# Reordering a batch's matrix products, joining cosine and sine, and moving stores to GpSimd's queue in an attention-and-mixer kernel

## The chip, the cores and the metric

The kernel runs on one core of a Trainium2 chip. The metric is the device time of one execution in microseconds, lower is better. An engine executes its own instructions in the order in which they stand in its queue, and waits for other engines and for transfers by semaphores. TensorE is called PE here (its weight loads PEld), VectorE DVE, ScalarE ACT, GpSimd POOL and SyncE SP.

## The reference

```python
kv  = einsum('bhsd,bhse->bhde', k, v)              # 8 batches, 8 heads, 576 tokens, 64
o   = einsum('bhsd,bhde->bhse', q, kv)
x   = o / sqrt(mean(o*o) + 1e-6) * g_norm          # -> (8, 576, 512)
th  = x @ w_theta
y   = w_tok_r @ (x*cos(th)) + w_tok_i @ (x*sin(th))   # along the tokens
u   = x + y
x   = u + relu(u @ w_ch)                            # first mixer
h   = relu(x.T @ w_tok1) @ w_tok2                   # along the tokens, 576 -> 256 -> 576
u   = x + h.T
out = u + relu(u @ w_ch1) @ w_ch2                   # 512 -> 1536 -> 512
```

## The kernel before

Products run in 16 bits with each operand split in a high and a low half, so each product is three matmuls (`mm3`, lines 82 to 84). There are two parts. The first goes batch by batch and ends with `u` of each batch in DRAM (`u2d`); the second (`mlp`) reads it back and does the last two products for eight chunks.

In the first part a batch passes through units, each a Python generator. `go(unit)` first moves every unit in flight one `yield` further, then starts the new one, so the source order is a software pipeline written out by hand. A planner then sets each engine's queue from this order by a simulated timeline, the earlier instruction in the program first.

The units, by name: `kv(o, part)` (product k,v in two parts), `attend(o, r)` for five row tiles r (q times kv on PE; square on ACT, sum on DVE, `pow` and a product on POOL, a product and a split on ACT and DVE, then a DMA transpose through SP), `rotate(o, r)` (x times w_theta on PE, then sine and cosine on ACT and the products and splits `zh`, `zl` on DVE; `rotate_last` for the last 64 tokens), `mix(o, c, dt)` (27 matmuls; c is one of two token chunks of 256 and 320 columns, dt one of four channel tiles; DVE adds the result to `R`, line 422, ACT writes the high half `uh`, line 423, DVE the low half `ul`, line 426), `channel(o, c, ct)` (12 matmuls on `uh` and `ul` of all four dt of its chunk; DVE adds to `R`, line 446, ACT and DVE split to `xs`, and after every second one SP issues a DMA transpose to `xt`, line 457), `token1(o, j, part)` (6 or 8 matmuls of 512 columns on `xt`; ReLU split to `hh` and `hl`), `token2(o, c, dt)` (6 matmuls; DVE adds to `R`, line 489, and after the last dt SP stores `R` to `u2d`, line 491). `weight` and `stash` prepare weights: `stash` loads four blocks of w_ch1 or w_ch2, decodes float64 words (`decode`), forms sums of blocks on POOL, splits them on ACT and DVE and stores them through SP (line 218). There are 24 stashes, handed out by `spare`, five in a round.

The order of a round of one batch (batches 2 to 5) was: eight `mix` units with the next batch's `attend` 2 to 4 and all five `rotate` among the first seven, eight `channel` units, the next-but-one batch's first `kv` part, four `token1` units, the second `kv` part, eight `token2` units with `attend` 0 and 1 of the next-but-one batch. Below, a unit is named by a letter and its indices: M for mix, C for channel, H for token1 and T for token2 (M13 is chunk 1, tile 3; H10 is part 1, j 0), K00 and K10 for the two kv parts, a2 for attend 2, r3 for rotate 3. The functions that the change touches, with the line numbers of the profile:

Of the kernel before, what the change touches and what calls it, by code (L numbers as in the profile page):

```python
# [10 lines left out]
F16 = mybir.dt.float16  # L11
# [17 lines left out]
def attn_mixer_kernel(  # L29
# [88 lines left out]
    def decode(val, raw, inplace=False):  # L118
# [6 lines left out]
        to = raw[..., 0] if inplace else bits  # L125
        nc.vector.scalar_tensor_tensor(to, raw[..., 0], 29, bits, ALU.logical_shift_right, ALU.bitwise_or)
        nc.vector.scalar_tensor_tensor(to, raw[..., 1], -(2**31), to, ALU.bitwise_and, ALU.bitwise_or)

    def weight(pool, w, row, col, part, n, hi, lo, scale, name, raw=None):

        val = pool.tile([P, n], F32, tag="val", name=f"{name}v")[:part]
        rows = slice(row, row + part)
        if w.dtype == F32:
            load(val, w[rows, col:col + n])
            yield
        else:
            if raw is None:
                raw = pool.tile([P, n, 2], I32, tag="raw", name=f"{name}r")[:part]
                load(raw.rearrange("p n w -> p (n w)"), w.bitcast(I32)[rows, 2 * col:2 * (col + n)])
            yield  # L140
            yield from decode(val, raw)
        if w is not w_theta and w is not w_ch1:
# [9 lines left out]

    def weight_tile(pool, w, pr, j, n, scale, name, col=0, raw=None):
        at = slice(col, col + n)
        return weight(pool, w, j * P, col, P, n, pr[0][:, j, at], pr[1][:, j, at], scale, f"{name}{col}_{j}", raw)
# [26 lines left out]
    def stash(w, name, rows, cols, dst):  # L182
# [4 lines left out]
        words = () if w.dtype == F32 else (2,)  # L187
        raw = wp[0].tile([P, 4, P, *words], I32 if words else F32, tag="raw", name=f"{name}r")
        t = wp[0].tile([P, 4, P], F32, tag="val", name=f"{name}s")
        for half, at in ((0, slice(0, 4, 3)), (1, slice(1, 3))):  # L190
            src = (w.bitcast(I32) if words else w)[rows[half]:rows[half] + P, :]
            n = 2 if words else 1
            src = src.rearrange("p (a n) -> p a n", a=2)[:, :, n * cols:n * (cols + P)]
            load(raw[:, at].rearrange("p a n w -> p a (n w)") if words else raw[:, at], src)
# [3 lines left out]
        val = raw  # L198
        if words:

            yield from decode(t.rearrange("p x n -> p (x n)"), raw.rearrange("p x n w -> p (x n) w"), True)
            val = raw[..., 0].bitcast(F32)
        yield

        nc.gpsimd.tensor_tensor(t[:, 1], val[:, 3], val[:, 2], ALU.add)
        nc.gpsimd.tensor_tensor(t[:, 3], val[:, 3], val[:, 0], ALU.subtract)
        nc.gpsimd.tensor_tensor(t[:, 2], t[:, 1], val[:, 0], ALU.subtract)
        nc.gpsimd.tensor_tensor(t[:, 0], val[:, 1], t[:, 2], ALU.subtract)
        nc.scalar.activation(hi[:, :3], val[:, :3], AF.Copy, scale=SW)
        yield  # L210
        nc.vector.scalar_tensor_tensor(lo[:, :3], val[:, :3], SW, hi[:, :3], ALU.mult, ALU.subtract)
        yield
        nc.scalar.activation(hi[:, 3:], t, AF.Copy, scale=SW)
        yield
        nc.vector.scalar_tensor_tensor(lo[:, 3:], t, SW, hi[:, 3:], ALU.mult, ALU.subtract)
        yield
        for d, src in zip(dst, (hi, lo)):
            nc.sync.dma_start(d, src)

    def stash_wide(g, k):  # L220
        return stash(w_ch1, f"wa{g}{k}_", (k * P, (DH + k) * P), g * P, [t[:, g, k] for t in wad])

    def stash_narrow(g, m):
        return stash(w_ch2, f"wb{g}{m}_", (g * P, (KH + g) * P), m * P, [t[:, g, m] for t in wbd])
# [112 lines left out]
    def rotate(o, r):  # L337
# [10 lines left out]
        f = fp.tile([P, DM], F32, tag="f", name=f"f{b}{r}", bufs=2)  # L348
        sn = fp.tile([P, DM], F32, tag="sn", name=f"sn{b}{r}", bufs=2)
# [6 lines left out]
        absolute(f)  # L356
        yield
        nc.scalar.activation(f, f, AF.Sin, bias=hpi, scale=-RAD)
        parts = ((sn, NR + r), (f, r))
        for t, kk in parts:  # L360
            mul.tensor_tensor(t, t, x, ALU.mult)
        yield
        for t, kk in parts:
            nc.scalar.activation(zh[:, kk, :], t, AF.Copy)
        yield
        for t, kk in parts:
            nc.vector.tensor_tensor(zl[:, kk, :], t, zh[:, kk, :], ALU.subtract)  # L367

    def rotate_last(o, xt):
# [7 lines left out]
        f = fp.tile([P, DM], F32, tag="f", name=f"f{b}{NR}", bufs=2)[:, :KD * SR].rearrange("p (k t) -> p k t", k=KD)  # L377
        sn = fp.tile([P, KD, 2, SR], F32, tag="sn", name=f"sn{b}{NR}", bufs=2)
# [6 lines left out]
        absolute(f)  # L385
        yield
# [14 lines left out]
    def mix(o, c, dts):  # L401
        b, R = o.b, o.R
# [17 lines left out]
        for dt, acc in zip(dts, py):  # L420
            u = R[:, dt, cols]
# [3 lines left out]
        for dt in dts:  # L425
            nc.vector.scalar_tensor_tensor(ul[:, dt, :], R[:, dt, cols], 1.0 / SW, uh[:, dt, :], ALU.mult, ALU.subtract)  # L426

    def channel(o, c, ct):
# [4 lines left out]
        if ct == 0:  # L433
# [3 lines left out]
            xs = tk[0].tile([P, KD, (tiles + 2) * P], F16, tag=f"xs{c}", name=f"xs{b}{c}")  # L437
            xt = tk[0].tile([P, KD * (tiles + 2), P], F16, tag=f"xt{c}", name=f"xt{b}{c}")
            o.x2.append((xs, xt))
        uh, ul = o.u[c]  # L440
        xs, xt = o.x2[c]
# [4 lines left out]
        nc.vector.scalar_tensor_tensor(x2, pr, 0.0, x2, ALU.max, ALU.add)  # L446
        nc.scalar.activation(xs[:, ct, :n], x2, AF.Copy, scale=1.0 / SW)
# [4 lines left out]
        for dst, at in lows:  # L452
            nc.vector.scalar_tensor_tensor(xs[:, ct, dst], x2[:, at], 1.0 / SW, xs[:, ct, at], ALU.mult, ALU.subtract)

        if ct % 2:
            m = tiles + 2
            nc.sync.dma_start_transpose(
                xt[:, (ct - 1) * m:(ct + 1) * m, :], xs[:, ct - 1:ct + 1, :].rearrange("p k t -> p (k t)")
            )

    def token1(o, j, part):
# [7 lines left out]
        xt = o.x2[part][1].rearrange("p (k r) d -> p r k d", k=KD)  # L469
# [6 lines left out]
        if part:  # L476
# [3 lines left out]
            split_relu(o.hh[:, j, :], o.hl[:, j, :], o.ph[j])  # L480
        yield

    def token2(o, c, dt):
# [6 lines left out]
        if dt == KD - 1:  # L490
            nc.sync.dma_start(u2d[:, :, b * S + cols.start:b * S + cols.stop], R[:, :, cols])
# [368 lines left out]
```

## Time and profile before

| | |
|---|---|
| median of 3 runs | 1177.35 us (1174.48 to 1177.61) |
| the profiled execution | 1177.31 us, span 1175.5 us, 1.8 us around it |
| PE busy | 1089.8 us, 93% |
| DVE busy | 849.6 us, 72% |
| ACT busy | 562.5 us, 48% |
| POOL busy | 236.3 us, 20% |
| HBM read and written | 74.29 MB and 29.88 MB |

All times in windows count from the start of the span. The part by batches ends at about 680 us, `mlp` follows. A round of batches 2 to 5 is the time from one batch's first `token2` add to the next batch's; the four rounds begin at 232, 310.3, 391.7 and 470.7 us. A granted clock of 1.00 is TensorE at 2.4 GHz; at 0.50 it runs at 1.2 GHz.

### The profile page before, as it was taken

How to read it: one execution, taken by the hardware profiler on the slowest of the kernel's cores; microseconds unless marked ns; L12 is line 12 of the kernel's file. 1: busy time of each engine (PE TensorE's matmuls, PEld its weight loads, DVE VectorE, ACT ScalarE, POOL GpSimd, SP SyncE). 2: the span in 40 equal slices, each digit the busy share in tenths (PEclk: the TensorE clock that was granted, in tenths of full speed). 3: DMA queues.
4: the chain of work that ended last, by engine and by line, in shares of the span. 5: the costliest groups of instructions: out<-in, count | busy, mean ns of one | idle time of the engine just before them, and what ended most of it. 6: DMA issues, size and time to landing. Idle time of an engine off the chain costs nothing.

```text
span 1175.5 us, 21915 instructions
## 1 busy us (share of the span) xinstructions
PE 1089.8 (93%) x8884; PEld 820.7 (70%) x8884; DVE 849.6 (72%) x1579; ACT 562.5 (48%) x1002; POOL 236.3 (20%) x258
## 2 busy tenths in 40 slices
PE   4759899898997997989999999999999999999998
PEld 3446666576665765767686777777777777777777
DVE  3997869798597696895955386857768584848583
ACT  2765645455264363462633163545536272626361
POOL 3774135072351450722400000000000000000000
PEclk9779999999998999999999999999999999999999
DMA  9616464592674666736273540101020202011101
GB/s 321 214 59 135 98 208 115 150 230 68 195 175 106 191 156 156 199 86 166 61 195 100 166 168 31 52 26 56 11 71 11 72 4 78 2 42 40 37 6 41
DMA packets 156357, 126.37 MB, mean 107 GB/s; under 512 B 93216, under 2 KB 137120, under 8 KB 156256
## 3 DMA queue, kind: packets, MB, share of 16 engines
q1 hardware_dynamic: 156256, 124.98, 38.0%
q8 instruction: 69, 1.13, 0.4%
q14 instruction: 32, 0.26, 0.1%
HBM read 74.29 MB, written 29.88 MB: 89 GB/s over the span
## 4 chain that ended last, share of the span: by engine, by line
PE 39%; DVE 36%; DMA 13%; ACT 4%; POOL 3%; issue 3%; SPq 2%; DVEq 0%; ACTq 0%; POOLq 0%
DMA xt<-xs 4%; PE na L82 3%; PE na L84 3%; PE na L83 3%; DVE gl L553 3%; DVE zl L367 3%; DVE gl L601 2%; DMA c<-u2d 2%; PE pa L82 2%; ACT gh L552 2%; PE pa L83 2%; PE pa L84 2%; PE pr L83 2%; DMA wa_r<-in_w_ch 1%; PE pr L84 1%
## 5 line engine op out<-in xcount | busy, mean ns | idle before, releaser
L82 PE MATMUL py<-wmh,zh 128*128 128x256 f16 (+1 forms) x576 | 166.8, 290 | 8.6 <-DMA zh<-zt 4.8
L83 PE MATMUL py<-wml,zh 128*128 128x256 f16 (+1 forms) x576 | 166.6, 290 | 0.0
L84 PE MATMUL py<-wmh,zl 128*128 128x320 f16 (+1 forms) x512 | 147.7, 289 | 5.3 <-DVE zl L367 5.3
L82 PE MATMUL na<-gh,wbh 128*128 128x288 f16 x384 | 106.7, 286 | 9.6 <-DVE c L612 9.6
L83 PE MATMUL pa<-o,wah 128*128 128x288 f16 x384 | 109.4, 286 | 0.0
L83 PE MATMUL na<-gl,wbh 128*128 128x288 f16 x384 | 109.1, 286 | 0.0
L84 PE MATMUL na<-gh,wbl 128*128 128x288 f16 x384 | 109.0, 286 | 0.0
L82 PE MATMUL pa<-o,wah 128*128 128x288 f16 x384 | 108.6, 286 | 0.2 <-DVE pre L595 0.2
L84 PE MATMUL pa<-o,wal 128*128 128x288 f16 x384 | 108.5, 286 | 0.0
L612 DVE SCALAR_TENSOR_TENSOR c<-na,c 128x288 f32<-128x288 f32 x64 | 28.5, 456 | 79.9 <-PE na L84 79.9
L82 PE MATMUL pr<-uh,wch 128*128 128x256 f16 (+1 forms) x256 | 76.3, 298 | 9.7 <-ACT uh L423 9.6
L83 PEld LDWEIGHTS <-wbh 128*128 128x128 f16 x672 | 65.7, 98 | 27.1 <-issue 10.7
L553 DVE TENSOR_TENSOR gl<-sum,gh 128x1152 f16<-128x1152 f32 x48 | 65.1, 1356 | 24.3 <-ACT gh L552 23.4
L83 PE MATMUL pr<-ul,wch 128*128 128x256 f16 (+1 forms) x256 | 76.2, 298 | 5.5 <-DVE ul L426 5.5
L83 PEld LDWEIGHTS <-wah 128*128 128x128 f16 x672 | 65.7, 98 | 17.7 <-issue 1.1
L82 PEld LDWEIGHTS <-wah 128*128 128x128 f16 x672 | 65.7, 98 | 16.6
L82 PEld LDWEIGHTS <-wbh 128*128 128x128 f16 x672 | 65.7, 98 | 16.6
L84 PEld LDWEIGHTS <-wbl 128*128 128x128 f16 x672 | 65.7, 98 | 16.6
L84 PEld LDWEIGHTS <-wal 128*128 128x128 f16 x672 | 65.7, 98 | 16.6
L84 PE MATMUL pr<-uh,wcl 128*128 128x256 f16 (+1 forms) x256 | 76.2, 298 | 0.0
L82 PEld LDWEIGHTS <-zh 128*128 128x128 f16 x576 | 57.1, 99 | 26.0 <-DMA zh<-zt 5.4
L302 POOL TENSOR_TENSOR ri<-ss,mhalf 128x8 f32<-128x8 f32 x40 | 71.4, 1785 | 2.0
(315 smaller groups left out, 2980.9 us busy)
## 6 DMA issues: line engine op xcount, KB each, us to landing
q<-in_q SPq DMA_DIRECT2D x8, 1152.0 KB, 7.2
c<-u2d SPq DMA_DIRECT2D x32, 288.0 KB, 4.4
out<-c SPq DMA_DIRECT2D x64, 144.0 KB, 1.8
k<-in_k SPq DMA_DIRECT2D x24, 256.0 KB, 4.8
v<-in_v SPq DMA_DIRECT2D x24, 256.0 KB, 5.1
wa_r<-in_w_ch SPq DMA_DIRECT2D x24, 256.0 KB, 3.9
wb_r<-in_w_ch SPq DMA_DIRECT2D x24, 256.0 KB, 3.8
wad<-wa SPq DMA_DIRECT2D x24, 224.0 KB, 2.1
```

The costliest lines, as they stand in the source:

```text
L82: nc.tensor.matmul(acc, ah, bh, start=first and i == 0, stop=False, **more)
L83: nc.tensor.matmul(acc, ah, bl, start=False, stop=False, **more)
L84: nc.tensor.matmul(acc, al, bh, start=False, stop=last and i == n - 1, **more)
L302: nc.gpsimd.tensor_tensor(ri, ss, mhalf, ALU.pow)
L367: nc.vector.tensor_tensor(zl[:, kk, :], t, zh[:, kk, :], ALU.subtract)
L552: nc.scalar.activation(h.hi[:, 3:], h.s, AF.Copy)
L553: nc.vector.tensor_tensor(h.lo[:, 3:], h.s, h.hi[:, 3:], ALU.subtract)
L601: nc.vector.tensor_tensor(h.lo[:, :3], h.own, h.hi[:, :3], ALU.subtract)
L612: nc.vector.scalar_tensor_tensor(dst, acc, 1.0 / SW**2, dst, ALU.mult, ALU.add)
```

## The change

It does five things. It lists the units of a round in a table: the first chunk's channel units stand among the second chunk's mix units, K00 before the second chunk's channel units, r3 among the `token1` units, r4 after C03, a0 and a1 of the next-but-one batch a little earlier; in the last batch, the units of batch 6 and 7 are interleaved in another order, and batch 1 has its own list. It puts cosine and sine in one tile `cs`, so that the product with x and the two splits are one instruction each, and takes the absolute value on ACT (`AF.Abs`) and not on DVE. It marks mix's and channel's follow-up instructions and the ReLU split as `urgent`, with a precedence of 120 instructions in the planner. It issues the stores of `stash` and of `token2` from POOL, the latter two units later. And `stash` decodes into a tile `t` of its own (one buffer) and splits all seven blocks with one ACT and one DVE instruction; the tile `xs` of `channel` becomes three smaller buffers; w_tok2 is loaded in four pieces, not six.

```diff
-    def absolute(t):
-        t = t.bitcast(I32)
-        nc.vector.tensor_scalar(t, t, 2**31 - 1, None, ALU.bitwise_and)
+    def urgent():
+        return tc.high_priority(offset=120)
...
 def stash
+        t = wp[0].tile([P, 8, P], F32, tag="st", name=f"{name}s", bufs=1)
+            yield from decode(t[:, :4].rearrange("p x n -> p (x n)"), raw.rearrange("p x n w -> p (x n) w"))
...
-        nc.scalar.activation(hi[:, :3], val[:, :3], AF.Copy, scale=SW)
-        nc.vector.scalar_tensor_tensor(lo[:, :3], val[:, :3], SW, hi[:, :3], ALU.mult, ALU.subtract)
-        nc.scalar.activation(hi[:, 3:], t, AF.Copy, scale=SW)
-        nc.vector.scalar_tensor_tensor(lo[:, 3:], t, SW, hi[:, 3:], ALU.mult, ALU.subtract)
+        nc.scalar.activation(hi, t[:, 1:], AF.Copy, scale=SW)
+        nc.vector.scalar_tensor_tensor(lo, t[:, 1:], SW, hi, ALU.mult, ALU.subtract)
...
         for d, src in zip(dst, (hi, lo)):
-            nc.sync.dma_start(d, src)
+            nc.gpsimd.dma_start(d, src)
...
 def rotate
+        cs = fp.tile([P, 2, DM], F32, tag="cs", name=f"cs{b}{r}", bufs=2)
+        f, sn = cs[:, 0], cs[:, 1]
...
         nc.scalar.activation(sn, f, AF.Sin, scale=-RAD)
-        absolute(f)
-        yield
+        nc.scalar.activation(f, f, AF.Abs)
         nc.scalar.activation(f, f, AF.Sin, bias=hpi, scale=-RAD)
-        parts = ((sn, NR + r), (f, r))
-        for t, kk in parts:
-            mul.tensor_tensor(t, t, x, ALU.mult)
-        yield
-        for t, kk in parts:
-            nc.scalar.activation(zh[:, kk, :], t, AF.Copy)
-        yield
-        for t, kk in parts:
-            nc.vector.tensor_tensor(zl[:, kk, :], t, zh[:, kk, :], ALU.subtract)
+        yield
+        mul.tensor_tensor(cs, cs, x.unsqueeze(1).to_broadcast([P, 2, DM]), ALU.mult)
+        yield
+        at = slice(r, r + NR + 1, NR)
+        nc.scalar.activation(zh[:, at, :], cs, AF.Copy)
+        yield
+        nc.vector.tensor_tensor(zl[:, at, :], cs, zh[:, at, :], ALU.subtract)
...
 def mix
-            nc.vector.tensor_tensor(u, acc, u, ALU.add)
+        with urgent():
+            nc.vector.tensor_tensor(u, py[0], u, ALU.add)
             nc.scalar.activation(uh[:, dt, :], u, AF.Copy, scale=1.0 / SW)
         yield
+        with urgent():
             nc.vector.scalar_tensor_tensor(ul[:, dt, :], u, 1.0 / SW, uh[:, dt, :], ALU.mult, ALU.subtract)
...
 def token2
         if dt == KD - 1:
-            nc.sync.dma_start(u2d[:, :, b * S + cols.start:b * S + cols.stop], R[:, :, cols])
+            yield
+            yield
+            nc.gpsimd.dma_start(u2d[:, :, b * S + cols.start:b * S + cols.stop], R[:, :, cols])
...
+    MIX, CHANNEL, TOKEN2 = ([f"{k}{c}{i}" for c in range(2) for i in range(KD)] for k in "MCT")
+    TOKEN1 = [f"H{c}{i}" for c in range(2) for i in range(KJ)]
...
+    def run(units, o, nxt, after, beside):
+        for u in units:
+            kind, c, i = u[0], int(u[1]), int(u[2])
+            if kind == "K":
+                front(kv, after, c)
+            else:
+                go(UNITS[kind](o, c, i))
+            for what in beside.get(u, "").split():
+                ...
+    TOKENS1 = ["K00", "H00", "H01", "K10", "H10", "H11"]
+    STEADY = MIX[:6] + CHANNEL[:2] + MIX[6:] + CHANNEL[2:4] + ["K00"] + CHANNEL[4:] + TOKENS1[1:] + TOKEN2
+    BESIDE = {
+        "M00": "a2", "M01": "a3", "M02": "a4 l", "M03": "r0", "M10": "w", "M11": "r1", "M12": "r2", "M13": "w",
+        "C03": "r4", "C11": "w", "H01": "r3", "H11": "n0 w", "T01": "n1", "T10": "w",
+    }
...
+        elif b == 1:
+            run(MIX[:4], o, nxt, None, {})
+            run(TOKENS1 + TOKEN2, before, None, nxt, {"H11": "n0", "T01": "n1", "T10": "w"})
+            run(MIX[4:6] + CHANNEL[:1], o, nxt, None, {"M10": "a2", "M11": "a3", "C00": "a4 l"})
+            after = loaded[0]
+            run(STEADY[STEADY.index("C01"):], o, nxt, after, {
+                "C01": "r0", "M12": "r1", "M13": "r2", "C03": "r4", "C11": "w", "H01": "r3", "H11": "n0 w", "T01": "n1", "T10": "w",
+            })
...
+            run(MIX[:6], o, None, None, {"M00": "f", "M01": "f", "M02": "f", "M03": "f"})
+            run(TOKEN1, before, None, None, {})
+            run(CHANNEL[:2] + MIX[6:], o, None, None, {})
+            run(TOKEN2[:4], before, None, None, {})
+            run(CHANNEL[2:] + TOKEN1[:2], o, None, None, {})
+            run(TOKEN2[4:], before, None, None, {})
+            run(TOKEN1[2:] + TOKEN2, o, None, None, {})
```

In the table, `a` and `r` are attend and rotate of the next batch, `n` attend of the next-but-one, `w` a stash or weight unit, `l` the loads of the next-but-one batch. `run` hands each to the same `front`, `go` and `spare` as before.

## Rows read from the trace of the kernel before

**Rows 1.** The page: the span, and each engine's busy time.

```profile
span 1175.5 us, 21915 instructions
...
PE 1089.8 (93%) x8884; PEld 820.7 (70%) x8884; DVE 849.6 (72%) x1579; ACT 562.5 (48%) x1002; POOL 236.3 (20%) x258
```

**Rows 2.** Windows: busy us (instructions) of PE, PEld, DVE, ACT, POOL; clock; DMA; GB/s.

```profile
0.00:120.00 120.00, 82.37 (x631) 60.18 (x631) 93.97 (x137) 68.11 (x122) 67.17 (x61) 0.86 0.59 181
120.00:232.00 112.00, 101.30 (x882) 70.92 (x880) 86.44 (x189) 58.84 (x126) 31.60 (x37) 0.95 0.55 145
232.00:310.30 78.30, 72.70 (x603) 51.59 (x601) 62.11 (x121) 37.99 (x73) 31.43 (x37) 0.96 0.65 161
310.30:391.70 81.40, 74.78 (x606) 52.36 (x605) 63.65 (x121) 38.57 (x73) 29.18 (x36) 0.94 0.59 155
391.70:470.70 79.00, 72.40 (x612) 51.92 (x610) 62.63 (x121) 37.99 (x73) 28.89 (x35) 0.98 0.61 160
470.70:549.00 78.30, 72.91 (x616) 52.61 (x614) 64.17 (x126) 38.76 (x74) 30.21 (x37) 0.98 0.56 141
549.00:680.00 131.00, 130.88 (x1029) 97.54 (x1028) 80.27 (x165) 50.65 (x97) 17.83 (x19) 1.00 0.51 147
```

**Rows 3.** Waits of PE in the four rounds, 232 to 549: total us, times, longest.

```profile
PE pr L82 <- ACT uh L423: 9.6, 4, 2.5
PE pr L83 <- DVE ul L426: 5.5, 7, 1.1
PE ph L473 <- DMA xt<-xs: 4.9, 4, 1.9
PE kvp L268 <- DMA v<-in_v: 3.4, 4, 1.5
```

**Rows 4.** Waits of PE between 120 and 232.

```profile
PE py L82 <- DMA zh<-zt: 3.7, 1, 3.7
PE kvp L268 <- DMA v<-in_v: 2.1, 1, 2.1
PE pu L82 <- ACT hh L75: 2.1, 2, 1.6
PE ph L473 <- DMA xt<-xs: 1.6, 1, 1.6
```

**Rows 5.** Windows within the second round, columns as in the second group.

```profile
340.00:362.00 22.00, 22.00 (x200) 16.11 (x199) 22.00 (x40) 14.73 (x28) 7.08 (x9) 1.00 0.38 108
...
373.00:392.00 19.00, 16.90 (x157) 10.30 (x156) 7.21 (x16) 3.85 (x8) 2.09 (x4) 0.91 0.79 196
```

**Rows 6.** Timeline, second round: M13's last matmul on PE; its add on DVE.

```profile
355.66 0.30 PE L84 MATMUL py<-wmh,zh 128*128 128x320 f16 x1
...
365.40 0.48 DVE L422 TENSOR_TENSOR R<-py,R 128x320 f32<-128x320 f32 x1
```

**Rows 7.** Timeline of PE, second round: C13's end, H00 and H01, H10's start.

```profile
374.96 0.30 PE L84 MATMUL pr<-uh,wcl 128*128 128x320 f16 x1
...
376.27 0.39 PE L473 MATMUL ph<-xt,w1h 128*128 128x512 f16 x1
...
378.66 0.38 PE L475 MATMUL ph<-xt,w1l 128*128 128x512 f16 x1
...
382.44 0.43 PE L473 MATMUL ph<-xt,w1h 128*128 128x512 f16 x1 [0.95 <-DMA xt<-xs]
```

**Rows 8.** Timeline of SP there: the last channel transpose.

```profile
377.31 2.50 SPq L457 DMA_TRANSPOSE xt<-xs  x1
```

**Rows 9.** DVE groups in the four rounds: busy us, mean ns, idle before.

```profile
L361 DVE TENSOR_TENSOR sn<-sn,x 128x512 f32<-128x512 f32 x16 | 11.8, 739 | 0.0
...
L72 DVE TENSOR_SCALAR f<-f 128x512 int32<-128x512 int32 (+1 forms) x20 | 10.1, 506 | 0.0
```

**Rows 10.** The same of DVE between 20 and 90.

```profile
L72 DVE TENSOR_SCALAR f<-f 128x512 int32<-128x512 int32 (+1 forms) x5 | 4.7, 946 | 0.0
```

**Rows 11.** Waits of SP's queue in the four rounds.

```profile
SPq L218 <- ACT wa L213: 32.4, 9, 10.4
...
SPq L218 <- ACT wb L213: 24.8, 8, 7.3
```

More of the change, by code (lines that the diff above doesn't have):

```diff
@@ L451, in channel, with token1 @@
             lows.append((slice(n, tiles * P), slice(2 * P, n)))
[L452 to L461, printed above, removed]
+        with urgent():
+            for dst, at in lows:
+                nc.vector.scalar_tensor_tensor(xs[:, ct % 2, dst], x2[:, at], 1.0 / SW, xs[:, ct % 2, at], ALU.mult, ALU.subtract)
+            if ct % 2:
+                m = tiles + 2
+                nc.sync.dma_start_transpose(
+                    xt[:, (ct - 1) * m:(ct + 1) * m, :], xsf
+                )
+    def token1(o, part, j):
         b = o.b
@@ L737, in attn_mixer_kernel @@
-    before, stashing = None, False
+    MIX, CHANNEL, TOKEN2 = ([f"{k}{c}{i}" for c in range(2) for i in range(KD)] for k in "MCT")
+    TOKEN1 = [f"H{c}{i}" for c in range(2) for i in range(KJ)]
+    UNITS = {"M": mix, "C": channel, "H": token1, "T": token2}
+    def run(units, o, nxt, after, beside):
[3 more added lines that the diff above has]
+                front(kv, after, c)
+            else:
+                go(UNITS[kind](o, c, i))
+            for what in beside.get(u, "").split():
+                if what == "w":
+                    spare()
+                elif what == "l":
+                    if o.b + 2 < B:
+                        loaded.append(load_heads(o.b + 2))
+                elif what[0] == "a":
+                    front(attend, nxt, int(what[1]))
+                elif what[0] == "n":
+                    front(attend, after, int(what[1]))
+                elif what[0] == "r":
+                    front(rotate, nxt, int(what[1]))
+                elif what == "f":
+                    next(first, None)
@@ L742, in attn_mixer_kernel @@
         if b == 0:
-            attends, rotations = {0: 0, 1: 1, 2: 2, 3: 3, 4: 4}, {4: 0, 5: 1, 6: 2, 9: 3, 10: 4}
-        elif b == 1:
-            attends, rotations = {4: 2, 5: 3, 6: 4}, {6: 0, 7: 1, 9: 2, 11: 3, 13: 4}
-        for i in range(2 * KD):
-            if i == KD and before is not None:
-                narrow_tokens(before, nxt)
-                if nxt is not None:
-                    widen_tokens(before, nxt)
-                    before = None
-            go(mix(o, i // KD, (i % KD,)))
-            if i in attends:
-                front(attend, nxt, attends[i])
-            if i == max(attends) + 1 and b + 2 < B:
-                after = load_heads(b + 2)
-            if i in rotations:
-                front(rotate, nxt, rotations[i])
-            if b == 0 or b > 1 and i in (0, 2, 5):
-                spare()
-            if b == B - 1 and i % 2:
-                next(first, None)
@@ L764, in attn_mixer_kernel @@
-        if b == 0:
+            run(MIX, o, nxt, None, {
+                "M00": "a0 w", "M01": "a1 w", "M02": "a2 w", "M03": "a3 w", "M10": "a4 r0 w", "M11": "r1 l w", "M12": "r2 w", "M13": "w",
+            })
+            after = loaded[0]
             spare(len(extra))
@@ L770, in attn_mixer_kernel @@
             extra += [weight_tile(wp[0], w_tok1, w1, j, DT, SW, "w1") for j in range(NR)]
-            extra += [weight(wp[0], w_tok1, SM, 0, SR, DT, w1rh[:SR], w1rl[:SR], SW, "w1r")]
-            extra += [
-                weight_tile(wp[0], w_tok2, w2, j, S // 3, SW, "w2", col) for j in range(KJ) for col in range(0, S, S // 3)
-            ]
-        for i in range(2 * KD):
-            go(channel(o, *divmod(i, KD)))
-            if 2 * KD + i in rotations:
-                front(rotate, nxt, rotations[2 * KD + i])
-            spare(1 if b == 0 else 0)
-        if b == 0:
+            src, _ = words(w_tok1)
+            extra += [weight(wp[0], w_tok1, src[SM:], SR, DT, w1rh[:SR], w1rl[:SR], SW, "w1r")]
+            extra += [weight_tile(wp[0], w_tok2, w2, j, S // 2, SW, "w2", col) for j in range(KJ) for col in range(0, S, S // 2)]
+            run(CHANNEL, o, nxt, after, {
+                "C00": "w", "C01": "r3 w", "C02": "w", "C03": "r4 w", "C10": "w", "C11": "w", "C12": "w", "C13": "w",
+            })
             spare(len(extra))
```

143 lines of the change are left out of this document (69 added, 74 removed).

## The prediction, before the kernel ran

> **What bounds the kernel now.** I read the page first: PE is busy 1089.8 of 1175.5 us, DVE 72%, ACT and POOL far less [rows 1]. So the kernel is a PE kernel, and what an order of units can win is PE's idle time and the time in which PE ran at the lower clock. The windows by stage say where these lie [rows 2]. From 549 to 680 PE is busy 130.88 of 131 us at clock 1.00: nothing is to be won in the last two batches, and the second part is not touched. In the four rounds of batches 2 to 5 PE is idle 5.6, 6.6, 6.6 and 5.4 us, 24.2 us in all. The granted clock there is 0.96, 0.94, 0.98 and 0.98; work that ran at half speed counts as busy, so I take (1 - clock) times busy as its price: 2.9 + 4.5 + 1.4 + 1.5 = 10.3 us. The same two figures are 10.7 and 5.1 us between 120 and 232 (batch 0's channels, batch 1). Before 120 PE is idle 37.6 us; there DVE is busy 94 us.
>
> Then I asked the waits what PE was idle for in the rounds [rows 3]: 9.6 us for `uh` and 5.5 for `ul` (the inputs of the channel products, C10 on), 4.9 for the transposed `xt` ahead of `token1`, 3.4 for v. That is 23.4 of the 24.2 us. Two causes stand behind these. The first is DVE: between 340 and 362 it is busy 22.00 of 22 us [rows 5], and M13's add comes at 365.40 although its last matmul began at 355.66 [rows 6]: 9.7 us late, behind the rotations' and a stash's instructions in the queue. The second is that from 373 to 392, with the channel, token and kv units, DVE has 7.21 us of work in 19 [rows 5], while C13's result goes round DVE, ACT, DVE and a transpose: from C13's last matmul at 374.96 to H10's start at 382.44 [rows 7] are 7.5 us, with H00 and H01 alone to cover it, the transpose issued at 377.31 [rows 8].
>
> **The change part by part.** *Order and precedence.* C00 now stands behind M11, so M03's `uh` and `ul` have M10 and M11 as cover: 54 matmuls of 320 columns. 512 columns take (378.66 - 376.27)/11 = 0.217 us [rows 7], so 320 take 0.136 by columns, an estimate, and the cover is 7.3 us. C10 has behind M13 the 24 matmuls of C02 and C03 (0.109 each by columns, 2.6 us), r4's and K00's. What it needs is add, high and low half, three instructions of about 0.5 us each like the add [rows 6], 1.5 us, if they don't queue behind rotations; the precedence is for that. I take all of the 15.1 us for `uh` and `ul` as gone. The instructions pushed back by the precedence are rotations and stashes: zl of r3, the latest, is due in M00 of the next round. From H01 to there stand H10 and H11 (16 matmuls of 0.217, 3.5 us) and eight T units (48 of about 0.12, 5.9 us), over 9 us, against a chain of some eight instructions of 0.6 to 0.8 us (0.74 for a DVE product [rows 9]); a delay of 3 us costs nothing.
>
> K00 stands ahead of C10, so v's loads have 48 matmuls (6.5 us) more: the 3.4 us go. H00 needs the transpose after C03; between them stand C10 to C13, 6.5 us, and K00 and r4. H10 needs the one after C13: 7.5 us, against H00, H01 (2.6) and r3 (12 matmuls of the same width, 2.6), so 5.2 us without K10. That leaves a wait between 0 and 2.3 us a round; I take 1.0, as SP no longer has v's loads in front. With 1 us for `hh` and what I don't see, 2.0 us of idle stays of some 6 in a round: 24.2 - 8 = 16.2 us won. The lower clock followed the idle stretches (1.00 before the gap, 0.91 behind it [rows 5]), so I let its price shrink in proportion: 10.3 x 16.2/24.2 = 6.9 us.
>
> Against this, DVE's work moves into the token stage. A whole round has 62 to 64 us of DVE [rows 2] in what would be 72 us or so of PE. r3, two stashes and two attends now lie beside C1, H and T, where T's adds free the banks that the next T needs, and T has no precedence. The bounds are nothing and the 2.5 us of the longest wait for DVE's lateness before [rows 3]; I take 1 us a round, 4 us.
>
> *Cosine and sine.* The 20 absolute values of the rounds cost DVE 10.1 us [rows 9], 2.5 a round; they go to ACT, at its mean instruction of 0.52 us (37.99/73) 2.6 us on top of 38 in 78 [rows 2], hidden. The joined products and splits have the same columns, so I take nothing for them. In the rounds all this is in the figures above: it lowers DVE from 63 to about 60.6 us. At the start DVE itself is the limit: five absolute values cost 4.7 us between 20 and 90 [rows 10]. Bounds 0 to 4.7; I take 3 us, as part of DVE's time there waits for ACT.
>
> *The stores.* SP stood 57.2 us in the four rounds before a stash's store for ACT alone [rows 11], with loads and transposes queued behind it. These waits move to POOL: 2 x 5 stash stores and 2 of `R` a round. Queued behind them are the attends' `pow` and product. The trace has no store issued by POOL. POOL's mean instruction is 0.85 us (31.43/37) [rows 2]; the bounds for one are nothing and 2.5 us, what SP took over that transpose [rows 8]. At 0.85, twelve take 10 us on top of 29 to 31 of 78. a2 stands at M00 and r2 behind M12, so an attend has 6 mix units in between: I take nothing for it on the path.
>
> The Trainium skill, "DMA: Bandwidth & Descriptors", section "Issuing engines are not separate DMA queues", says that another issuing engine saves only the usually small issue time. By it the stores' move would be worth nothing by itself; the 57.2 us show a queue that stands rather than one that is slow, but PE waited on SP's order only in the 8.3 us for `xt` and v that I have counted already. The sum is the same by both, save that the H10 wait would be its upper bound, 2.3 us, 5 us more in all.
>
> *120 to 232.* Batch 1 has its own list with the old order for its first half. The waits for v and `xt` (3.7 us) go as in the rounds, those for `hh` (2.1) by two thirds (1.4); the 3.7 us for `zt` stay, as r4 of batch 0 now starts a unit later [rows 4]. So 5.1 of 10.7 us, and of the clock's 5.1 us in proportion 2.4: 7.5 us.
>
> *The rest*: stash's single `t`, with five stashes in 78 us and some five instructions each, I take at nothing; the last batches' order at nothing, with no idle time before it [rows 2].
>
> **The sum.** 16.2 + 6.9 - 4 + 7.5 + 3 = 29.6 us off 1177.31, the profiled execution's own time, which is 0.04 us from the median: 1148 us.
>
> **The rivals.** *A, the waits move on:* the precedence makes `uh` timely, but with DVE at 60 in 72 us the backlog comes out at the next users: H10 at 2.3 us, T's banks at 2.5 us, each round. Then a round keeps 4.8 of its 6 us idle, 1.3 x 4 = 5 us won, with 2 of clock; with 7 us from the rest of the first part it gives about 1163. For it speaks DVE's full window [rows 5]; against it, that the DVE time behind that window is nearly empty.
>
> *B, no change:* the units' order was not the limit, and the planner lays DVE's queue much as before; 1174 to 1180. The add that is 9.7 us late [rows 6] speaks against it.
>
> *C, the stores slow DVE (slower):* the absolute value took 946 ns beside a POOL busy 67 of 120 us, and 506 where POOL was busy 29 to 31 of 78 [rows 2, 9, 10]. So an active POOL stretches DVE, up to 1.87 times. If each of the twelve stores cost DVE d, DVE would need 60.6 + 12 d a round and becomes the longest engine from d = 0.9 us (about 71.5 us of PE at full clock: 72.91 less 1.5). At the 2.5 us bound of a store, stretched 1.87 times (12 x 2.5 x 0.87/1.87 = 14 us lost), DVE needs 74.6 us and its waits at the head and tail of a round, some 7 us of its present 16 idle, stay: 81.5 against 79.2, 9 us more over four rounds, about 1186 with nothing won elsewhere. Against it: POOL's present 30 us a round stretch the average product to 739 ns only [rows 9]. The Trainium skill's page "SBUF — State Buffer", section "SBUF: two separate sides", names the converse as a trap: stores issued by GpSimd stand while DVE holds a shared port, and it advises another queue. No run here yet shows a store from POOL.
>
> **How the numbers follow.** The forecast has 0.52, all idle and slow clock of the rounds gone 0.06 (34.5 + 12 + 3 off, down to 1128), A 0.17, B 0.09, C with other losses 0.16. The forecast's own range is 1138 to 1158: the H10 wait at either bound, T's price from 0 to 2.5 us a round, the start from 0 to 4.7. To hold 8 in 10 the range goes through A and the near half of B: 1131 to 1178. A change under 0.3%, 3.5 us, can't be told from none here (the three runs span 3.1 us): faster 0.75, same 0.09, slower 0.16.
>
> **What would show it.** Right: in the rounds PE's waits for `uh` and `ul` are gone, clock 0.99 or 1.00, a round of 72 to 74 us; M13's add follows its matmuls within 3 us; DVE below 61 us a round; the `xt` wait before H10 about 1 us. Wrong: PE waits for `zl`, for a T unit's bank, or for `zh<-zt`; DVE's products grow beyond 0.74 us; POOL stands in front of a store while x is due; the `zt` wait in batch 1 grows.

## The result, and the profile of the changed kernel

The changed kernel is slower: 1187.19 us (median of 4 runs, 1186.02 to 1187.72) against 1176.79 for the kernel before beside it, a ratio of 1.009 [1.0073, 1.0108]. The forecast was 1148, the range ended at 1178.

The page of the changed kernel, span and busy time [rows 1]:

```profile
span 1185.8 us, 21685 instructions
PE 1091.3 (92%) x8884; PEld 823.1 (69%) x8884; DVE 824.4 (70%) x1449; ACT 570.6 (48%) x980; POOL 258.6 (22%) x316
```

PE's work is nearly the same, 1091.3 us against 1089.8; DVE has 25 us less to do. So 8.8 of the 10.3 us of span are idle time, and the rest is a little clock. The windows by stage, changed kernel, columns as in [rows 2]:

```profile
0.00:120.00 120.00, 83.29 (x630) 60.23 (x631) 88.62 (x128) 72.63 (x127) 65.21 (x57) 0.86 0.59 181
120.00:232.00 112.00, 102.08 (x894) 73.44 (x892) 79.16 (x153) 58.39 (x117) 31.89 (x40) 0.95 0.58 145
232.00:310.00 78.00, 68.81 (x569) 48.32 (x566) 53.40 (x97) 35.02 (x63) 31.75 (x45) 0.93 0.58 148
310.00:392.00 82.00, 72.71 (x597) 51.49 (x598) 60.72 (x104) 39.65 (x71) 35.15 (x48) 0.96 0.65 160
392.00:470.00 78.00, 71.89 (x612) 52.13 (x611) 61.05 (x105) 40.09 (x72) 34.34 (x49) 0.98 0.62 166
470.00:549.00 79.00, 73.73 (x620) 53.56 (x619) 60.35 (x105) 39.33 (x71) 33.85 (x47) 0.96 0.62 140
549.00:680.00 131.00, 128.46 (x1005) 95.04 (x1004) 83.83 (x158) 50.54 (x91) 26.39 (x33) 1.00 0.55 152
```

In the rounds PE is idle 29.9 us where it was 24.2, while DVE fell from 252.6 to 235.5 us. In the 22 us that end 4 to 7 us behind M13's last matmul DVE is busy 16 to 18 us in each round, where it was 20 to 22: it is no longer full, and still PE waits. The waits of PE there, 232 to 549, answer to [rows 3]:

```profile
PE pr L82 <- ACT uh L424: 14.6, 4, 5.0
PE ph L477 <- DMA xt<-xs: 8.0, 5, 3.3
PE pu L82 <- DVE R L494: 3.9, 4, 1.2
PE pr L83 <- DVE ul L427: 2.4, 2, 1.2
```

The waits for v are gone. Those for `uh` and `ul`, 15.1 us before, are 17.0: fewer and longer, once a round and up to 5 us. Those for `xt` rose from 4.9 to 8.0, and a wait for a T unit's bank (`R`) is new.

By PE's timeline, from landmark to landmark (before, then after): up to batch 1's first T unit 228.11 and 227.66; the four rounds, to that of batch 5, 315.84 and 320.01; from there to the second part's first matmul 122.68 and 124.66; the second part 508.87 and 513.47. That is -0.45, +4.17, +1.98 and +4.60 us, in sum the 10.3.

The round from 228 to 311 shows what stands in the way. C10 needs M13's `uh`. M13's last matmul starts at 275.37, its add at 285.90: 10.5 us late, as in [rows 6]. Timelines of SP, ACT, DVE and PE, changed kernel:

```profile
275.37 0.30 PE L84 MATMUL py<-wmh,zh 128*128 128x320 f16 x1
...
276.31 1.46 SPq L461 DMA_TRANSPOSE xt<-xs  x1
277.82 1.95 SPq L116 DMA_DIRECT2D wa_r<-in_w_ch  x2
...
281.80 0.30 PE L84 MATMUL pr<-uh,wcl 128*128 128x320 f16 x1
...
282.79 0.66 ACT L121 ACTIVATE wa_s<-wa_r 128x512 f32<-128x512 f32 x1 [3.85 <-DMA wa_r<-in_w_ch]
...
283.48 0.43 DVE L123 TENSOR_SCALAR wa_s<-wa_s 128x512 int32<-128x512 int32 x1 [3.24 <-ACT wa_s L121]
...
285.90 0.48 DVE L423 TENSOR_TENSOR R<-py,R 128x320 f32<-128x320 f32 x1
...
286.64 0.45 ACT L424 ACTIVATE uh<-R 128x320 f16<-128x320 f32 x1
...
287.14 0.42 PE L82 MATMUL pr<-uh,wch 128*128 128x320 f16 x1 [5.05 <-ACT uh L424]
```

SP issues a stash's load behind a channel transpose. The decode of that stash (L121 on ACT, L123 on DVE) heads both queues until the load has landed; ACT stands 3.85 us and DVE 3.24 with nothing else to show. Behind it, in order, stand r2's rotation and M13's add. In the three rounds that follow M13's last matmul starts at 358.46, 440.22 and 516.85. DVE's timeline there, the decode and the add:

```profile
364.25 0.43 DVE L123 TENSOR_SCALAR wa_s<-wa_s 128x512 int32<-128x512 int32 x1 [2.70 <-ACT wa_s L121]
...
366.05 0.48 DVE L423 TENSOR_TENSOR R<-py,R 128x320 f32<-128x320 f32 x1
...
442.59 0.43 DVE L123 TENSOR_SCALAR wb_s<-wb_s 128x512 int32<-128x512 int32 x1 [1.72 <-ACT wb_s L121]
...
445.68 0.48 DVE L423 TENSOR_TENSOR R<-py,R 128x320 f32<-128x320 f32 x1
...
521.13 0.43 DVE L123 TENSOR_SCALAR wb_s<-wb_s 128x512 int32<-128x512 int32 x1 [3.08 <-ACT wb_s L121]
...
524.21 0.48 DVE L423 TENSOR_TENSOR R<-py,R 128x320 f32<-128x320 f32 x1
```

So the add is 10.5, 7.6, 5.5 and 7.4 us late in the four rounds, 7.7 in the mean; in the kernel before it was 7.8, 9.7, 8.9 and 8.9, in the mean 8.8. The round shown first is the worst. The wait of 1.7 to 3.2 us is a part of this; the rest is mostly the instructions of rotations, of the stash and of M12 that stand ahead of the add. Over the four rounds ACT's waits for these loads are:

```profile
ACT wa_s L121 <- DMA wa_r<-in_w_ch: 25.5, 7, 6.0
...
ACT wb_s L121 <- DMA wb_r<-in_w_ch: 16.5, 8, 3.9
```

42.0 us. The kernel before had 52.2 of them, but 33.3 of these in four waits of 7.5 to 8.9 us, one at the end of each round's `token1` (the second from 376.3 to 385.2), where DVE had 7.21 us of work in 19 [rows 5] and no product waited.

### The profile page after: what moved, and what is told of

The parts are those of the page before. It is cut to its first block, busy times and chain, and to the rows that moved or that the text cites. A ratio compares the mean times of both kernels' runs of the same rounds, so it can differ in the third digit from the quotient of the medians.

```text
span 1185.8 us, 21685 instructions
## 1 busy us (share of the span) xinstructions
PE 1091.3 (92%) x8884; PEld 823.1 (69%) x8884; DVE 824.4 (70%) x1449; ACT 570.6 (48%) x980; POOL 258.6 (22%) x316
## 3 DMA queue, kind: packets, MB, share of 16 engines
q1 hardware_dynamic: 140608, 104.53, 33.3%
## 4 chain that ended last, share of the span: by engine, by line
PE 32%; DVE 31%; DMA 16%; ACT 9%; POOL 6%; issue 3%; SPq 3%; DVEq 0%; ACTq 0%; POOLq 0%
DMA xt<-xs 5%; PE na L82 3%; PE na L84 3%; PE na L83 3%; DVE gl L560 3%; DMA c<-u2d 2%; DVE gl L608 2%; DMA wa_r<-in_w_ch 2%; DMA wb_r<-in_w_ch 2%; DVE cs L363 2%; PE pa L82 2%; ACT gh L559 2%; PE pa L84 2%; PE pa L83 2%; DVE zl L368 2%
## 5 line engine op out<-in xcount | busy, mean ns | idle before, releaser
L82 PE MATMUL pr<-uh,wch 128*128 128x256 f16 (+1 forms) x256 | 76.2, 300 | 15.5 <-ACT uh L424 15.5
L83 PEld LDWEIGHTS <-wbh 128*128 128x128 f16 x672 | 66.0, 98 | 27.9 <-issue 11.2
```

The lines of the kernel that those rows point to most:

```text
L82: nc.tensor.matmul(acc, ah, bh, start=first and i == 0, stop=False, **more)
L83: nc.tensor.matmul(acc, ah, bl, start=False, stop=False, **more)
```

## The experiments

All are timed beside the kernel before on the same chip. "Rounds" is the time between the first T units of batch 1 and batch 5, "u" PE's waits for `uh` and `ul` and "decode" ACT's waits for a stash's load, both from 232 to 549, all three of the one profiled execution (0: none listed). Single executions of one kernel lie up to 15 us apart, so a profile's figure is no mean: e11's profiled execution took 1166.2 us, the fastest of its ten. The runs were timed in groups, and the kernel before had medians from 1175.4 to 1177.6 in them; where two runs of different groups are compared, the difference of their ratios is the fairer figure (0.001 is 1.2 us).

| run | units' order | precedence | stores | other | us, median | ratio to before | rounds | u | decode |
|---|---|---|---|---|---|---|---|---|---|
| before | old | none | SP | | 1175.4 to 1177.6 | 1 | 315.8 | 15.1 | 52.2 |
| after | new | all | POOL | | 1187.2 | 1.009 [1.0073, 1.0108] | 320.0 | 17.0 | 42.0 |
| e1 | new | all | SP | | 1179.9 | 1.0044 [1.0026, 1.0061] | 318.2 | 13.0 | 43.8 |
| e2 | new | none | POOL | | 1171.1 | 0.9966 [0.9953, 0.9979] | 307.3 | 12.5 | 24.8 |
| e3 | new | all | POOL | decode 3 steps later | 1183.5 | 1.0064 [1.0045, 1.0084] | 316.2 | 14.2 | 37.1 |
| e4 | new | all | POOL | cosine, sine apart | 1186.0 | 1.0085 [1.0064, 1.0106] | 316.3 | 11.8 | 33.7 |
| e5 | old | all | POOL | | 1186.9 | 1.0086 [1.0056, 1.0117] | 318.5 | 2.1 | 25.2 |
| e6 | new | all | POOL | M13's stash to T02 | 1177.8 | 1.0003 [0.9985, 1.0022] | 313.6 | 6.9 | 18.8 |
| e7 | new | none | SP | | 1179.3 | 1.0038 [1.0017, 1.006] | 313.5 | 20.9 | 37.2 |
| e8 | new | none | SP | M13's stash to T02 | 1173.5 | 0.9976 [0.9956, 0.9997] | 304.1 | 9.7 | 19.3 |
| e9 | old | none | POOL | | 1187.4 | 1.0101 [1.0079, 1.0122] | 318.7 | 3.4 | 34.0 |
| e10 | new | none | POOL | M13's stash to T02 | 1176.2 | 0.9999 [0.9978, 1.0021] | 309.6 | 2.8 | 17.5 |
| e11 | new | mix only | POOL | | 1173.4 | 0.9972 [0.9949, 0.9995] | 305.5 | 12.5 | 23.0 |
| e12 | new | C and H only | POOL | | 1186.5 | 1.0083 [1.0058, 1.0107] | 319.0 | 16.0 | 40.7 |
| f1 | new | none | SP | code of before | 1181.6 | 1.0061 [1.0042, 1.008] | 318.0 | 14.2 | 42.0 |
| f2 | new | all | POOL | stash loads on POOL | 1176.5 | 1.0018 [0.9995, 1.0042] | 309.8 | 7.8 | 0 |
| f3 | old | none | POOL | code of before | 1193.1 | 1.0155 [1.0131, 1.0179] | 331.9 | 0 | 38.4 |
| f4 | new | mix only | POOL | stash loads on POOL | 1176.6 | 1.0012 [0.9986, 1.0037] | 308.2 | 7.1 | 0 |
| g1 | old | none | SP | | 1175.4 | 0.9984 [0.9973, 0.9995] | 310.4 | 9.7 | 33.9 |
| g2 | new | none | POOL | code of before | 1193.1 | 1.0128 [1.0111, 1.0145] | 322.4 | 20.7 | 36.5 |

### Which part costs: stores, precedence, decode, cosine

Four runs undo one thing each in the changed kernel.

```diff
 e1 (stash and token2)
-            nc.gpsimd.dma_start(d, src)
+            nc.sync.dma_start(d, src)
 e2 (urgent)
-        return tc.high_priority(offset=120)
+        return ExitStack()
 e3 (stash, between load and decode)
-        for _ in range(4):
+        for _ in range(7):
 e4 (rotate and rotate_last: absolute value on DVE, products and splits one by one)
-        nc.scalar.activation(f, f, AF.Abs)
+        absolute(f)
```

> The changed kernel (1187.2 us) with the stores of stash and of token2 issued by SP again. Theory L (late loads): in each round a stash's decode stands in ACT's and DVE's queues ahead of M13's add and waits 2.4 to 3.9 us for its load, which SP issues behind a channel transpose; the stores have no part in it, so 1184 to 1192 us and PE's wait for uh stays at 12 to 19 us. Theory S (the stores on POOL stretch DVE or hold up the attends): the time falls to 1178 or below, and DVE's mean product gets shorter.

> The changed kernel without the precedence of 120 instructions, all else kept. Theory L: the queue in front of M13's add is set by when the planner believes the loads to land, not by precedence, so 1184 to 1191 us with the uh wait within 12 to 19 us. Theory U (the precedence itself displaced rotations and stashes into worse places): 1172 to 1182. If the precedence does what the prediction said, it gets slower: 1193 or more.

> The changed kernel with seven steps instead of four between a stash's load and its decode. Theory L: the loads have landed when their decode comes to the head of the queue, ACT's waits for wa_r and wb_r fall from 51 us in all to under 15, PE's wait for uh from 15.5 to under 6, and the time to 1170 to 1179 us. Theories S and U: the uh wait stays above 12, 1184 to 1190 us.

> The changed kernel with cosine and sine as before (absolute value on DVE, products and splits one by one; the tile stays joined). The prediction's term: DVE gets 2.5 us a round more, and the start 3 us, so 1188 to 1196 us. Theory V (the chain of sine, absolute value, cosine on ACT, and the product that waits for both, is what makes rotations late): faster, 1176 to 1184, with the waits for zt and the product gone.

The stores (e1) are worth 7 us, 5 by the ratios, between the two expectations. The absolute value and the joined products (e4) are worth 1.2 us, inside both intervals: nothing that can be told. Starting the decode three steps later (e3) took the decode waits only from 42.0 to 37.1, and `uh` and `ul` from 17.0 to 14.2; so the steps alone do not bring the load ahead of its use, and the run does not decide about the decode. The precedence (e2) is the large term: without it the kernel is 16 us faster, 15 by the ratios, just below theory U's range, and faster than the kernel before. That refutes the prediction's reason for it, that it takes the waits for `uh` away.

### Whose precedence

```diff
 e11 (channel, token1)          e12 (mix)
-        with urgent():         -        with urgent():
+        with ExitStack():      +        with ExitStack():
```

> The changed kernel with precedence for the mix units' add and uh and ul alone, none for the channel units' and token1's instructions. Theory Q1 (it is the adds of the mixing put ahead of attends and rotations that push the others back): 1182 to 1190. Rival Q2 (it is the channel's and token1's precedence that does it): 1169 to 1177.

> The changed kernel with precedence for the channel units' and token1's instructions alone, none for the mix units'. Theory Q1: 1167 to 1177, about the time without any precedence. Rival Q2: 1182 to 1190. If the two need each other, this and the run with the mix units' alone are both under 1178.

Q2 holds: with the mixing's precedence alone 1173.4, with the channel's and `token1`'s alone 1186.5. The 13 to 15 us (by the ratios) are the price of the second. In code, the channel's precedence covers SP's channel transposes too, since they stand in the same `with`; what these alone cost was not separated. By PE's timeline the four rounds took 83.1, 82.1, 77.4 and 77.5 us in the changed kernel and 76.7, 77.0, 76.2 and 77.6 in e2, so in these profiles the price lies in the first two. What the precedence does there is seen at one place of the first round, 20 to 22 us behind the first T unit (at 227.7 in the changed kernel, at 225.9 in e11). First the changed kernel, timelines of ACT and DVE:

```profile
248.56 0.68 ACT L121 ACTIVATE wa_s<-wa_r 128x512 f32<-128x512 f32 x1 [5.97 <-DMA wa_r<-in_w_ch]
249.14 0.40 ACT L424 ACTIVATE uh<-R 128x256 f16<-128x256 f32 x1
249.44 0.57 ACT L301 ACTIVATE x<-po 128x512 f32<-128x512 f32 x1
...
265.83 0.68 DVE L326 TENSOR_TENSOR xs<-x,xs 128x512 f16<-128x512 f32 x1
```

Then e11, the same two views:

```profile
245.62 0.63 ACT L330 ACTIVATE R<-xt 128x512 f32<-128x512 f16 x1 [1.65 <-DMA xt<-xs]
246.15 0.40 ACT L424 ACTIVATE uh<-R 128x256 f16<-128x256 f32 x1
246.46 0.58 ACT L301 ACTIVATE x<-po 128x512 f32<-128x512 f32 x1
247.25 0.68 ACT L121 ACTIVATE wa_s<-wa_r 128x512 f32<-128x512 f32 x1 [0.21 <-DMA wa_r<-in_w_ch]
...
256.55 0.68 DVE L326 TENSOR_TENSOR xs<-x,xs 128x512 f16<-128x512 f32 x1
```

With the channel's precedence the decode stands ahead of M01's `uh`, an attend's square (L301) and, next in line, a rotation's input (L330, 249.92), and ACT stands 5.97 us. In e11 it stands behind them and waits 0.21. The round's last attend starts its last step (L326) 38.2 us behind the first T unit against 30.7, and the rotations and M13's add follow that. But in the other three rounds this step comes at 34.1, 32.1 and 32.1 us, where in e11 it comes at 32.7 each time, and e6 below, 9 us faster, has it at 33.8 to 37.8. So the rows show that the decode stands there and what ACT waits for it; that the late attend is how the 13 to 15 us are paid, they do not show. Why the planner lays the decode there when channel units come first was not looked into. PE's waits in the rounds of e11:

```profile
PE pr L82 <- ACT uh L424: 11.2, 4, 4.0
...
PE ph L477 <- DMA xt<-xs: 1.2, 3, 0.7
```

`xt` falls from 8.0 to 1.2 and the T banks from 3.9 to 1.9 though the channel units, which make `xt`, have no precedence any more. `uh` stays at 11.2. PE's idle time in the rounds is 18.6 us in e11 against 29.9 in the changed kernel, and most of that difference is in these waits.

### The decode at the head of the queue

Two ways to take the decode out of M13's way: its stash is issued with T02 (e6 with all precedence, e8 and e10 without), or the stashes' loads are issued by POOL and so no longer stand behind SP's transposes (f2, f4).

```diff
 e6, e8, e10 (BESIDE)
-        "M00": "a2", ... "M13": "w", ... "T01": "n1", "T10": "w",
+        "M00": "a2", ... "T01": "n1", "T02": "w", "T10": "w",
 f2, f4 (stash; f4 on e11)
-            load(raw[:, x:x + 2] ...)
+            nc.gpsimd.dma_start(raw[:, x:x + 2] ...)
```

> Everything of the changed kernel stays (precedence too), but the stash unit that was issued with M13 is issued with T02. Theory Q (head of the queue): M13's add is late because the decode of that stash, waiting for its load, stands ahead of it on ScalarE and VectorE. Then PE's waits for uh in the four rounds fall from 14.6 us to under 7, and the time is 1172 to 1180 against 1187. Rival R (the plan is only reshuffled): another instruction takes that place, uh stays above 10 us, and the time is 1183 to 1190.

> Without the precedence, stores on SP, and M13's stash unit issued with T02. Theory Q: the decode ahead of M13's add is gone here as well; waits for uh in the rounds, 11.2 us without the precedence alone, fall under 5, and the time is 1158 to 1166. Rival R: 1168 to 1175, with uh waits above 8 us.

> Without the precedence, M13's stash unit issued with T02, stores on GpSimd as in the change. Theory Q (the decode that stands ahead of M13's add is a cost of its own, some 6 to 9 us): 1160 to 1167, with under 6 us of waits for uh in the rounds. Rival R (without the precedence the decode's place costs nothing more, the next wait takes over): 1168 to 1174.

> The changed kernel, all precedence kept, with the stash's loads issued by GpSimd instead of SP. Theory Q: the cost is the decode that waits for a load issued behind transposes. Then ScalarE's waits for these loads in the rounds fall from 42 us to under 20, PE's for uh from 14.6 to under 7, and the time is 1171 to 1179. Rival D: the background work is simply laid in a worse order; the loads' time doesn't matter, the waits for uh stay above 10 us and the time is 1183 to 1191. If GpSimd comes to the load later than SP did, the waits grow and it is over 1191.

> Precedence for the mixing alone, and the stash's loads issued by GpSimd. Theory Q: ScalarE's 23 us of waits for these loads and PE's 11.2 us for uh fall by half or more: 1160 to 1168. Rival D: 1170 to 1177 as with SP's loads.

Under the precedence both ways bring about the same, 9.4 us (e6) and 10.7 (f2), by the ratios 10 and 8, and both take `uh` and `ul` to 7 or 8 us. M13's add is 8.4, 2.1, 3.7 and 4.8 us late in e6's rounds, 6.0, 8.1, 7.2 and 2.6 in f2's, where ACT waits for no load at all: the decode's wait made the add later, but in f2 it is still 6.0 us late in the mean without one. `xt` is waited for more in both, 13 us. As e6 moves a whole stash unit and f2 all the loads, what M13's wait cost by itself is not shown; that the decodes' place and their loads are worth 8 to 11 us under the precedence is. Without the channel's precedence the same is worth 6 us in e8 (against e7; T's banks now take 10.0 us there), and brings nothing in e10 and f4, which are 3 to 5 us slower than e2 and e11 (e10 above both of its expectations): e10's `uh` is gone too, but H10's wait comes in its place, 13.9 of the 15.1 us that follow. PE in the rounds of e10 (in f4 it is 12.7 us, longest 4.8):

```profile
PE ph L477 <- DMA xt<-xs: 15.1, 7, 4.5
...
PE pr L82 <- ACT uh L424: 0.7, 1, 0.7
```

That is rival A of the prediction, the waits that move on. Theory Q is right on the place of the wait, and wrong where it took the wait for a cost that can simply be taken off.

### Order and the stores' queue

```diff
 e5, e9, g1 (old order in every batch; BESIDE and the first and last batches' lists likewise)
-    STEADY = MIX[:6] + CHANNEL[:2] + MIX[6:] + CHANNEL[2:4] + ["K00"] + CHANNEL[4:] + TOKENS1[1:] + TOKEN2
+    STEADY = MIX + CHANNEL + TOKENS1 + TOKEN2
 e7, g1: e1's and e2's edits; f1, g2: the kernel before with the new lists of units
 f3, g2 (on the code of before, stash and token2)
-            nc.sync.dma_start(d, src)
+            nc.gpsimd.dma_start(d, src)
```

> The units in the order of the kernel before, with the precedence and everything else of the change. Without the precedence this order took 1187.4, the new order 1171.1. If the precedence costs by itself what it cost in the new order (some 15 us): 1196 to 1204. If it costs only where the new order puts channel units between mix units: 1184 to 1190. If it helps the old order, where PE waited 20 us in the rounds for transposed xt: 1175 to 1183.

> Without the precedence, and with the units in the order of the kernel before; the joined cosine and sine, the stash in one piece and the stores on GpSimd stay. If the order of units is what brought the kernel without precedence to 1171 (the prediction's step, worth some 8 us of idle time), this is 1176 to 1184, and the waits for uh and ul together are above 15 us. If the rest did, the time is 1168 to 1173 and the order is worth nothing.

> Without the precedence and with the stores issued by SP again. By itself the first gave about 15 us, the second about 6. If the stores cost something of their own (GpSimd's queue or a stretched VectorE), the two add up: 1162 to 1168. If the stores cost only what the late queues under the precedence made of them, nothing is left: 1169 to 1174. If SP's queue stands in front of loads without the precedence, as it did in the kernel before (57 us of waits for stores): slower than 1174.

> The kernel before with the new order of units alone: rotations, stash, stores (SP) as before, no precedence. Theory O: the order is worth some 16 us wherever it stands, and the other parts of the change (joined cosine and sine, stash, stores) cost some 10 us by themselves: 1158 to 1166. Rival N: the order needs the lighter VectorE and GpSimd's stores that come with the change; here waits for uh and ul stay above 12 us in the rounds, and the time is 1170 to 1180.

> The kernel before with the stores of the stash and of token2 on GpSimd's queue, nothing else. If the stores are what makes the old order 10 us slower with the other parts of the change: 1182 to 1190. If another part does (stash in one piece, joined cosine and sine): 1170 to 1179, and the waits of SP for the stash's results, 57 us in the rounds, are gone without a gain on PE.

> The changed kernel without precedence, in the old order, with the stores on SP: only the joined cosine and sine, the new stash and smaller things are left of the change. Theory X (order and queue hang together: GpSimd's queue costs in the old order and saves in the new one): 1168 to 1178, against 1187.4 with the stores on GpSimd. Rival Y (the joined cosine and sine or the new stash is what the old order lost by): 1183 to 1190.

> The kernel before with the new order and the stores on GpSimd; rotations and stash as before, no precedence. Theory X: 1168 to 1176, some 8 us under the same with the stores on SP (1181.6), and near the 1171 of the changed kernel without precedence. Rival Y' (GpSimd's queue helps only beside the new stash and the joined cosine and sine): 1181 to 1195.

Without precedence order and queue are crossed twice:

| | stores by SP | stores by POOL |
|---|---|---|
| code of before, old order | 1176.8, 1 (before) | 1193.1, 1.0155 (f3) |
| code of before, new order | 1181.6, 1.0061 (f1) | 1193.1, 1.0128 (g2) |
| code of after, old order | 1175.4, 0.9984 (g1) | 1187.4, 1.0101 (e9) |
| code of after, new order | 1179.3, 1.0038 (e7) | 1171.1, 0.9966 (e2) |

By the ratios POOL's queue costs 18, 8 and 14 us in three pairs and saves 8 in the fourth. The new order costs 6 to 7 us with SP's stores; with POOL's it saves 16 in the code of after and 3, inside the intervals, in that of before. So nothing here has a worth of its own; the forecast's 16.2 us for the order were not to be had from the order alone (f1 is 5 us slower than before, 7 by the ratio). Theory X held for g1 and fell for g2. For e7 the third case came, slower than 1174. Three runs lie outside what was expected: e9 and f3 above it, f1 just above rival N's times. In e9 the waits for `uh` and `ul` are 3.4 us and not above 15; PE waits there 11.3 us for `xt` ahead of rotations and 9.1 ahead of `token1`. In e5 the precedence costs nothing (1186.9 against 1187.4): it hurts where the new order puts channel units between mix units.

Why POOL's queue costs in the old order is seen in f3. PE's largest wait there, and POOL ahead of it:

```profile
PE pt L82 <- DMA xt<-xs: 26.9, 7, 7.2
```

```profile
238.25 0.61 POOL L218 DMA_DIRECT2D wad<-wa  x1
238.81 0.27 POOL L301 TENSOR_TENSOR ss<-ss,eps 128x8 f32<-128x8 f32 x1
238.98 1.71 POOL L302 TENSOR_TENSOR ri<-ss,mhalf 128x8 f32<-128x8 f32 x1
240.60 0.61 POOL L218 DMA_DIRECT2D wad<-wa  x1
```

Stores and their waits stand between the steps of two attends (`pow` is L302). The first attend's product, L303, comes 16.4 us behind the round's first T unit; in the kernel before it came 9.4 behind it. The rotation that needs its transpose waits 7.2 us. In g2, with the new order, no such wait is listed; `uh` and `ul` take 20.7 us there, and why it loses as well is not shown. What in the new code lets the new order profit from POOL's queue (g2 against e2, 22 us apart, 19 by the ratios) stays open: the codes differ in the stash, the rotation, the buffers of `xs`, and in that the new code issues the stash's store one step and `u2d`'s two steps later, and these were not separated.

### The second part

Its code is unchanged but for the numbering of the stash's blocks, its matmuls are as many (4034), and it took 4.6 us more: 2.2 busy, 2.4 idle. The changed kernel's PE there:

```profile
1038.41 0.28 PE L82 MATMUL na<-gh,wbh 128*128 128x288 f16 x1 [1.95 <-DVE c L619]
1038.53 0.32 PE L83 MATMUL na<-gl,wbh 128*128 128x288 f16 x1
1038.65 0.43 PE L84 MATMUL na<-gh,wbl 128*128 128x288 f16 x1
```

and the same place in e2:

```profile
1023.26 0.28 PE L82 MATMUL na<-gh,wbh 128*128 128x288 f16 x1 [1.93 <-DVE c L619]
...
1023.50 0.28 PE L84 MATMUL na<-gh,wbl 128*128 128x288 f16 x1
```

The same gap of 1.9 us, the same work before it; in one the clock then falls to 1.2 GHz for 3.4 us, in the other it doesn't. Of the 20 profiled executions 11 have such a stretch in the second part. It goes with no part of the change, and is part of why executions of one kernel may differ; the 2.4 us of idle time were not traced to a cause.

## Why the prediction was wrong

- *"I take all of the 15.1 us for `uh` and `ul` as gone"*: this is the step that failed; 17.0 are left. For M13 it counted three instructions of 0.5 us, with the precedence to bring them forward, against the cover of C02, C03, r4 and K00. In the round shown PE had 6.3 us of such work and of C10's own first matmuls, up to the one at 281.80, and the add came 10.5 us late. It did not come within 3 us in any round, as it was to. What stood ahead of it, in place of a full DVE [rows 5], were the rotations' and the stash's instructions and, in every round, a decode that waited 1.7 to 3.2 us on DVE for its load. The lighter DVE brought the add from 8.8 us late to 7.7 in the mean and no further. Why an add with precedence still stands behind them stays open.
- *The lower clock, 6.9*: it was to shrink with the idle time, and that grew. By the prediction's own reckoning its price in the rounds is 12.1 us, where it was 10.3.
- *"a delay of 3 us costs nothing"*: the precedence was costed by the nine us between H01 and M00 of the next round. It cost 13 to 15, the mixing's share of it nothing that can be told (e2, e11, e12), in longer waits for `uh`, for `xt` and for T's banks; no wait for `zl` is listed among them.
- *The stores, "nothing on the path"*: 5 to 7 us in the changed kernel (e1). The sign listed for it, POOL in front of a store or an attend while x is due, is f3's. Rival C named a part that does cost, but the wrong mechanism: DVE's joined product takes 1245 ns beside POOL's stores and 1220 beside SP's (e1), and DVE's total fell. That its 1186 lies near the measured time is luck. The Trainium skill, "DMA: Bandwidth & Descriptors", section "Issuing engines are not separate DMA queues", counts only the small issue time in another engine's favour; here the issue took 0.57 us, and the move was worth from 18 us of loss to 8 of gain, by the order and the code around it.
- *120 to 232, 7.5*: came to 0.5 (from batch 1's first mixing matmul to its first T unit 94.8 us before, 94.3 after). The 10.7 us of idle time are 9.9: the waits for v and `xt` fell from 3.7 to 1.6, those for `hh` from 2.1 to 0.8 and `zt`'s from 3.7 to 2.9 [rows 4], but r4 in batch 1's list now waits 3.5 for `xt`, and the clock stayed at 0.95.
- *The start, 3*: nothing. DVE fell from 93.97 to 88.62 us before 120 [rows 2], and PE's first mixing matmul of batch 1 starts at 133.35 in both kernels.
- *H10's 1.0 us a round* measured 1.4 (0.3, 3.3, 2.2 and nothing listed), inside its bounds of 0 and 2.3. H00, taken at nothing, waited 1.3 and 0.9 us in two of the rounds. *T's 1 us a round* measured 0.97. *The v waits' 3.4* went. These last two terms held.
- *The last batches and the second part at nothing*: +2.0 (a T bank 1.2, `uh` 1.0, neither there before) and +4.6 (2.2 of it the lower clock, the idle 2.4 open).
- Of the rivals A was nearest in mechanism: waits moved on to T's banks (6.3 us in e6, 10.0 in e8) and to H10 (e6, f2, e10 and f4). It gave 1163 because it let `uh` be won first.

The kernels that beat both are e2 (0.9966), e11 (0.9972), e8 (0.9976) and, in the old order, g1 (0.9984): 2 to 4 us of the 29 forecast, and not from the steps that the forecast counted.

## What to carry to other kernels

When an instruction is late, list what stands ahead of it in its engine's queue, and count a waiting instruction there at its wait, not at its 0.5 us; a prefetch's consumer is the first to look at, since one decode of 0.7 us held two engines for up to 6. Then look at every round: the worst one is not the mean. A precedence has to be costed by what it pushes back and by where that then lands, and it is worth trying on one chain at a time. A part of a change that looks like an addition may cost 18 us or gain 8 by the others present, so cross the parts before you call one good.

## What the runs showed of the hardware

A store issued from POOL's queue took 0.57 us there (L221, 20 of `wad` and 20 of `wbd`), 0.75 for the larger `u2d`. `wad` and `wbd` landed 2.5 and 3.1 us after their issue where SP's, in the kernel before, took 2.1 and 2.2 (medians). DVE's joined product of 1024 columns took 1245 ns, one of 512 in e4 722, so joining saved 0.2 us a pair. After an idle gap of 1.9 us the clock fell in one execution and not in another, with the same work around it.
